# The last Q group's loads spread over stage 2, Wo copies two units later, and a weight ring that starts with five slots

## The chip, the core and the metric

The kernel runs on one core of a Trainium2 chip. The metric is the device time of one execution in microseconds; for the kernel before it is 2158.94 us, the median of six runs (2148.79 to 2162.49). The core has five engines with a queue each: TensorE (PE; its weight loads are listed as PEld), VectorE (DVE), ScalarE (ACT), GpSimd (POOL) and SyncE (SP). SP, ACT and POOL also issue DMAs, which run on 16 DMA engines that the three queues share.

## The reference

Two independent parts are computed, and their outputs stand side by side in the last dimension. Part A is a long convolution over the sequence, done with FFTs; part B is attention with a small memory that is carried from one segment of 32 positions to the next.

```python
# part A: B=1, S=2048, D=1024
kv  = shift_conv(k, shift_k) * v
y   = irfft(rfft(kv, 2S) * rfft(ssm_k, 2S))[:S]
a   = q * (y + kv * ssm_D)
# part B: Dm=1024, 32 heads of 128, memory of 8 rows
mem = mem0
for s in range(64):
    h = concat([mem, x[32*s:32*s+32]])               # 40 rows
    q, k, v = h @ Wq, h @ Wk, h @ Wv
    p = softmax(where(mask, q @ k.T * scale, -1e9))
    o = (p @ v) @ Wo
    mem, out[s] = o[:8], o[8:]
```

Each of Wq, Wk, Wv and Wo is 8 MB in bf16. They don't fit on the core together with what else is there, so a part of them is read again for every segment.

## The kernel before

**Weights in chunks.** The four matrices are cut into 64 chunks of 128 x 2048 (512 KB): eight chunks for each of two groups of K, Q and V, named (m, kc, g) with m = 0, 1, 2 and g = 0, 1, and sixteen of Wo, named (3, hp, 0). The 21 chunks of `STREAM` (L22) are streamed: early in the kernel they are copied to a scratch tensor WS in memory, and each of the 64 segments loads them from there through a ring of slots. The other chunks stay on the core (`res`). Six chunks of the last Q group, `kept_q1` (L431), get their place in the pool `pw` of eight 512 KB tiles, in tiles 4, 5, 6, 7, 0 and 1.

**Part A with part B's preparation inside it.** Stage 1 (L57 to L272) does the short convolution and the first DFT step and stores its results to SK1 and SU1. Stage 2 (L282 to L376) runs over 17 sets of rows, two halves each, 34 units in all. A set is read by four gathers on SP (`load_set` L304, tiles Kg and Ug, L289), one set ahead and with three buffers a tile; a unit then does matmuls, four products on DVE, one on POOL (Yre, L345), the inverse matmuls one unit later, and ACT stores the set to SZ (L297). Stage 3 (L378 to L399) reads SZ in 16 steps (zt) and writes part A's output.

After each unit of stage 2 and each step of stage 3 comes `fill()` (L647): it stores finished results to the scratch tensor REC (L641), issues one Wo copy from the weight to WS from unit `WO_COPY` on (L653 to L656, on POOL), one copy of other streamed chunks every second unit (L657), every third unit one block of x (`x_block`, L580: eight transposes on TensorE from X_sb, a copy on DVE into the tile xt, L589, and a store to REC on POOL, L590; a tile xt holds two blocks, so an even block's copy waits for the REC store of the block before), after every odd block the next X load (L576, on SP), and one slice of a dense projection (`dense`, L604) by `next(rest)` in two units out of three. The slices come from the generator `slices` (L619): 16 for group (0, 1), the second K group, 16 for (1, 0), the first Q group, 16 for (1, 1), the last Q group. When the generator turns to (1, 0), which is in unit 24, it issues the six loads of `kept_q1` on SP behind the last X load. Slices left over are done after stage 3, and then V's projection (L730 to L744), whose results go to the scratch tensor VBD from `vst` and `pair` tiles (L742).

**Order in the queues.** Up to the segments, a planner orders each engine's instructions at build time, by the order of the code and by when it holds an operand to be ready. `tc.issue_after(ins)` puts the instructions of a block behind `ins` on the same engine. In the segments (`tc.manual_schedule()`, L841) the order is that of the code.

**The ring.** `slot()` (L690) takes the first free of six slots; `fetch()` (L695) loads the next streamed chunk into it, on SP; `done(ch)` (L807), called after the last matmul on a chunk, frees its slot and fetches again. Slots 4 and 5 have memory of their own. Slots 0 to 3 share theirs with preparation: 0 and 1 with the transposed x (XBT), used to the end of V's projection, 2 and 3 with the `pair` tiles, of which wring2 is the one that V's last block is stored from. The order is `free = [4, 5, 0, 1, 3, 2]` (L688): two fetches stand ahead of V's projection (L727), `RING - 2` = 4 right before the segments (L842).

**A segment** does K, Q, K, Q, V, V projections of 40 rows (`Proj`, L916; the rows of x from REC), softmax, attention and Wo (`out_proj`, L1005), all from resident chunks and ring slots in the order of the chunks, and a transposition of the memory rows for the next segment. In segment 0 the streamed chunks 0 to 5 are (0,0,0), (0,1,0), (0,3,0), (0,7,0), (1,3,0) and (1,7,0); chunk 10 is (2,1,0) of V.

Of the kernel before, what the change touches and what calls it, by code (L numbers as in the profile page):

```python
# [23 lines left out]
TURN = (6, 4)  # L24
INLINE = {1: 0, 3: 1, 5: 0, 11: 1, 12: 0, 14: 1}
N2, N3 = 12, 15
WO_COPY = 27
X_LOAD, K_LOAD = 4, 2
RING = 6

PITCH = 2048


def a_kernel(ctx: ExitStack, tc, q, k, v, shift_k, ssm_k, ssm_D, outa, ps_sum, slot4, slot16, stage1_done, fill):
# [22 lines left out]
    with ExitStack() as c1:  # L57
# [183 lines left out]
        for t in range(16):  # L241
# [18 lines left out]
            for hf in range(2):  # L260
                cols = slice(512 * hf, 512 * hf + 512)
                ps = ps_sum.tile([128, 512], F32, tag="ps0", name="ks_ps")
                for li, lag in enumerate((3, 2, 1, 0)):
                    pr = wk.tile([128, 512], BF, tag="prod", bufs=10, name="prod")
# [17 lines left out]
    with ExitStack() as c2:  # L282
        gio = c2.enter_context(tc.tile_pool(name="a2_io", bufs=3, side="right"))
        wk = c2.enter_context(tc.tile_pool(name="a2_wk", bufs=3, side="right"))
        ps1 = c2.enter_context(tc.tile_pool(name="a2_ps", bufs=6, space=PSUM))

        def gather(dst, scratch, pr, eng):
            if pr <= 31:
                eng.dma_start(dst[:, :], scratch[4 * pr:4 * pr + 4].rearrange("m n d -> (m n) d"))  # L289
            else:  # L290
                eng.dma_start(dst[0:32, :], scratch[1])
                nc.gpsimd.memset(dst[32:64, :], 0.0)
                nc.gpsimd.memset(dst[64:128, :], 0.0)

# [9 lines left out]
        def load_set(st):  # L304
            prs = [2 * st, 2 * st + 1] if st < 16 else [32]
            Us, Ks = [], []
            for pi, pr in enumerate(prs):
                Kt_ = gio.tile([128, 1024], BF, tag=f"Kg{pi}", name="Kg")
                gather(Kt_, SK1, pr, nc.sync)
                Ut = gio.tile([128, 1024], BF, tag=f"Ug{pi}", name="Ug")  # L310
                gather(Ut, SU1, pr, nc.sync)
                Us.append(Ut)
                Ks.append(Kt_)
            return prs, Us, Ks
# [9 lines left out]
        def unit_front(st, prs, Us, Ks, hf):  # L324
            npart = 64 * len(prs)
            P_ = slice(0, npart)
            Kre_ps = fwd2(Ks, prs, Mre, hf, "Kre_ps")
            Kim_ps = fwd2(Ks, prs, Mim, hf, "Kim_ps")
            Kre = wk.tile([128, 512], BF, tag="Kre", name="Kre")
            Kim = wk.tile([128, 512], BF, tag="Kim", name="Kim")  # L330
            nc.scalar.copy(Kre[P_], Kre_ps[P_])
            nc.scalar.copy(Kim[P_], Kim_ps[P_])
            Ure_ps = fwd2(Us, prs, Mre, hf, "Ure_ps")
            Uim_ps = fwd2(Us, prs, Mim, hf, "Uim_ps")
            pa = wk.tile([128, 512], BF, tag="pa", name="pa")
            pb = wk.tile([128, 512], BF, tag="pb", name="pb")
            pc = wk.tile([128, 512], BF, tag="pc", name="pc")
            pd = wk.tile([128, 512], BF, tag="pd", name="pd")
            nc.vector.tensor_tensor(out=pa[P_], in0=Ure_ps[P_], in1=Kre[P_], op=ALU.mult)
            nc.vector.tensor_tensor(out=pb[P_], in0=Uim_ps[P_], in1=Kim[P_], op=ALU.mult)  # L340
            nc.vector.tensor_tensor(out=pc[P_], in0=Ure_ps[P_], in1=Kim[P_], op=ALU.mult)
            nc.vector.tensor_tensor(out=pd[P_], in0=Uim_ps[P_], in1=Kre[P_], op=ALU.mult)
            Yre = wk.tile([128, 512], BF, tag="Yre", name="Yre")
            Yim = wk.tile([128, 512], BF, tag="Yim", name="Yim")
            nc.gpsimd.tensor_tensor(out=Yre[P_], in0=pa[P_], in1=pb[P_], op=ALU.subtract)  # L345
            nc.vector.tensor_tensor(out=Yim[P_], in0=pc[P_], in1=pd[P_], op=ALU.add)
            return (Yre, Yim)
# [17 lines left out]
        for st in range(NS):  # L365
            cur = nxt
            if st + 1 < NS:
                nxt = load_set(st + 1)
            zss = [wk.tile([128, 1024], BF, tag=f"zs{pi}", name="zs") for pi in range(len(cur[0]))]
            for hf in range(2):  # L370
                Ys = unit_front(st, cur[0], cur[1], cur[2], hf)
                if pending is not None:
                    unit_back(*pending)
                pending = (st, cur[0], hf, Ys, zss)
                fill()
        unit_back(*pending)  # L376

    with ExitStack() as c3:  # L378
# [23 lines left out]
def b_kernel(ctx: ExitStack, tc, x, mem0, Wq, Wk, Wv, Wo, outb, n_seg, run_a):  # L402
# [28 lines left out]
    kept_q1 = own[1, 1][:6]  # L431
# [7 lines left out]
    def dram_chunk(ch):  # L439
        m, a, g = ch  # L440
        return Wo_v[a] if m == 3 else W_v[m][a, g]

    def dst_view(ap, ch):
        return ap.rearrange("p (hh d) -> p hh d", hh=2) if ch[0] == 3 else ap

    def stream_src(ch):
        return WS[ring_order.index(ch), :, 0:2048]
# [6 lines left out]
    res = {}  # L454
# [30 lines left out]
    def pw(k=None):  # L485
        if k is None:
            k = pw_next[0] % 8
            pw_next[0] += 1
        return pring.tile([128, 2048], BF, tag=f"pw{k}", name="pw")
# [64 lines left out]
    def group(m, g, temps={}, which=range(8), ws=None, eng=nc.sync, held=False):  # L554
        ws = ws or [None] * 8
        for kc in which:
            ch = (m, kc, g)
            if ch in res:
                got.append(eng.dma_start(res[ch], dram_chunk(ch)))
                ws[kc] = res[ch]  # L560
            else:
                t = temps[ch]() if ch in temps else pw()
                got.append(eng.dma_start(t[:], dram_chunk(ch)))
                if ch in streamed:
                    copies.append((stream_src(ch), t[:]))
                ws[kc] = t[:]
        while copies and not held:
            copied.append(nc.gpsimd.dma_start(*copies.pop(0)))
        return ws
# [23 lines left out]
    rec_stores, x_loads = [], []  # L593
# [24 lines left out]

    def slices():  # L619
        k1, q0 = group(0, 1, held=True), group(1, 0, held=True)  # L620
        q1 = [None] * 8
        first = [kc for kc in range(8) if (1, kc, 1) in kept_q1]
        rest = [kc for kc in range(8) if kc not in first]
        for m, g, ws in ((0, 1, k1), (1, 0, q0), (1, 1, q1)):
            if (m, g) == (1, 0):
                for ch, k in zip(kept_q1, (4, 5, 6, 7, 0, 1)):
                    res[ch] = pw(k)[:]
                assert not copies
                with tc.issue_after(x_loads[-1].ins):
                    group(1, 1, which=first, ws=q1)  # L630
            if (m, g) == (1, 1):
                group(1, 1, {(1, kc, 1): (lambda k=k: pw(k)) for kc, k in zip(rest, (2, 3))}, rest, q1)
            for _ in dense(m, g, ws):
                yield

    rest = slices()
    stores = []

    def store():
        if stores:  # L640
            nc.gpsimd.dma_start(*stores.pop(0))  # L641
# [2 lines left out]
    blocks = list(range(n_seg // 4))  # L644
    wo_copies = [ch for ch in ring_order if ch[0] == 3]

    def fill():  # L647
        store()
        n = units[0]
        units[0] += 1  # L650
        if n == 0:
            x_load(0)
        if n >= WO_COPY and wo_copies:  # L653
            ch = wo_copies.pop(0)
            with tc.issue_after(rec_stores[-1].ins):
                nc.gpsimd.dma_start(dst_view(stream_src(ch), ch), dram_chunk(ch))  # L656
        if n > 5 and n % 2 and copies:  # L657
            with tc.issue_after(rec_stores[-1].ins):
                copied.append(nc.gpsimd.dma_start(*copies.pop(0)))
        if n % 3 == 2 and blocks:  # L660
            b = blocks.pop(0)
            x_block(b)
            if b % 2 and blocks:
                x_load(b + 1)
        if n >= 34 or n % 3 != 2:
            next(rest, None)
# [18 lines left out]
             if s == 0 and ch not in v_temp[2:] or s > 0 and ch not in kept]  # L685
    live = {}
    now = [0]
    free = [4, 5, 0, 1, 3, 2]  # L688

    def slot():  # L690
        k = free.pop(0)
        t = (base if k < 4 else ring).tile([128, 2048], BF, tag=f"wring{k}", name="wring")
        return k, t

    def fetch():  # L695
        if loads:
            s, ch = loads.pop(0)
            live[s, ch] = k, t = slot()
            nc.sync.dma_start(t[:], stream_src(ch))
# [14 lines left out]
    with c0p:  # L714
# [15 lines left out]
        for g in range(2):  # L730
            ws = wv[g]
# [75 lines left out]
    def done(ch):  # L807
        if now[0] == 0 and ch in at_hand:
            place_late(1, at_hand[ch][1])
        elif ch in streamed:  # L810
            if now[0] == 0 and ch in kept:
                keep(ch)
            free.append(live.pop((now[0], ch))[0])
            i = order_s.index(ch)
            s, nxt = (now[0], order_s[i + 1]) if i + 1 < len(order_s) else (now[0] + 1, order_s[0])
            if nxt in kept and s > 0:
                unkeep(s, kept[nxt])
            else:
                fetch()
# [19 lines left out]
            tp[:, 0:256].rearrange("p (hf dq r) -> p dq hf r", hf=2, dq=4)[:, :, :, NX:SEG])  # L839

    with tc.manual_schedule():  # L841
        for _ in range(RING - 2):  # L842
            fetch()
        load_x(0)
        Y0 = one.tile([128, 256], BF, tag="PT", name="Y0")
# [49 lines left out]
        for s in range(n_seg):  # L895
# [143 lines left out]
            q1 = Proj(1, 1).run(4)  # L1039
# [4 lines left out]
            q1 = q1.run(4).evac()  # L1044
# [108 lines left out]
```

## Time and profile before

| What | us |
|---|---|
| median of six runs | 2158.94 |
| the profiled execution's own time | 2159.29 |
| its span, first to last instruction | 2157.5 |
| PE busy (81%) | 1752.0 |
| DVE / ACT / POOL busy | 866.4 / 637.3 / 430.0 |
| stage 2, rough window | 140 to 283 |
| stage 3, rough window | 283 to 347 |
| rest of the last Q group and V, rough window | 347 to 420 |
| segment 0, rough window | 420 to 456 |
| the other 63 segments | 456 to 2148 |

The DMA engines move 802.31 MB, 372 GB/s on the mean; 1215 ring fetches of 512 KB on SP are the largest part, with a median of 7.3 us from issue to landing. The mean granted TensorE clock is 0.98. A line of a timeline gives the start in us from the beginning of the span, the time from the first to the last of the merged instructions, the engine (SPq is SP's queue), the line of the kernel, the operation, what it writes and reads, the count, and in brackets how long the engine sat idle ahead of it and what ended that. A line of the waits gives who waited for whom, the total in us, how often, and the longest.

### The profile page before, as it was taken

Reading aid. Unit: us, or ns where it says so; the run is one execution under the profiler, and the core shown is the slowest. Engines: PE = TensorE matmul, PEld = TensorE weight load, DVE = VectorE, ACT = ScalarE, POOL = GpSimd, SP = SyncE. Lnnn points to the kernel's source line nnn. Section 1 sums busy time; section 2 is a strip of 40 time slices with the busy share of each in tenths; the row PEclk is TensorE's granted clock in tenths of the full one; section 3 lists DMA queues with packets and bytes.
Section 4 is the critical chain, followed back from the end, with each engine's and each line's share of the span. In section 5 each row is a group of like instructions: output and inputs, shape, how many; then the busy total and the mean of one; then the engine's idle time right before and its main releaser. Section 6 shows DMA issues by size and latency. Waiting matters only on the chain. (4 is left out here: it accounts for less than half of the span.)

```text
span 2157.5 us, 81579 instructions
## 1 busy us (share of the span) xinstructions
PE 1752.0 (81%) x35764; PEld 943.0 (44%) x35764; DVE 866.4 (40%) x2735; ACT 637.3 (30%) x1131; POOL 430.0 (20%) x1108
## 2 busy tenths in 40 slices
PE   6889879888888778878778888888888888887876
PEld 3433224344444444444444444444444444444444
DVE  9838652133333333333333333333333333333332
ACT  6936521122222222222222222222222222222221
POOL 3114522211111111111111111111111111111111
PEclk9999999989999999999999999999999999999999
DMA  8988989899999999999999999999999999999996
GB/s 305 370 326 309 320 297 376 289 397 392 392 389 391 384 381 389 382 389 384 377 388 394 386 385 376 389 388 382 388 386 388 391 389 390 393 392 388 386 390 266
DMA packets 238314, 802.31 MB, mean 372 GB/s; under 512 B 34722, under 2 KB 34754, under 8 KB 237956
## 3 DMA queue, kind: packets, MB, share of 16 engines
q1 hardware_dynamic: 206036, 724.01, 87.4%
q0 software_dynamic: 26704, 62.59, 8.4%
q10 hardware_dynamic: 5216, 10.49, 1.3%
q8 instruction: 280, 4.59, 0.9%
q14 instruction: 78, 0.64, 0.1%
HBM read 737.56 MB, written 62.39 MB: 371 GB/s over the span
## 5 line engine op out<-in xcount | busy, mean ns | idle before, releaser
L929 PEld LDWEIGHTS <-rec 128*32 128x32 bf16 x12351 | 325.8, 96 | 472.4 <-issue 253.9
L929 PE MATMUL acc<-wring,rec 128*32 128x512 bf16 x3765 | 377.1, 385 | 139.7 <-DMA wring<-WS 124.2
L938 ACT CAST qkv_sb<-acc 128x512 bf16<-128x512 f32 x384 | 224.8, 585 | 658.3 <-PE acc L929 655.2
L1015 PEld LDWEIGHTS <-OT 128*32 128x32 bf16 x8192 | 218.5, 97 | 172.7 <-issue 143.8
L1015 PE MATMUL yacc<-wring,OT 128*32 128x256 bf16 x3072 | 154.4, 278 | 92.5 <-DMA wring<-WS 54.2
L929 PE MATMUL acc<-Wmid,rec 128*32 128x512 bf16 x3072 | 227.5, 384 | 0.0
L929 PE MATMUL acc<-Wres,rec 128*32 128x512 bf16 x2816 | 221.2, 380 | 0.0
L875 PEld LDWEIGHTS <-OTB 128*16 128x16 bf16 x4096 | 103.9, 90 | 104.5 <-issue 94.8
L1001 ACT CAST OT<-OTp 128x512 bf16<-128x512 f32 x128 | 74.9, 585 | 244.6 <-PE OTp L993 244.4
L1031 DVE COPY KT<-tps 128x512 bf16<-128x512 bf16 x64 | 27.2, 425 | 293.5 <-PE tps L944 293.5
L1002 DVE CAST OTB<-OTp 128x128 bf16<-128x128 f32 x128 | 37.4, 292 | 263.0 <-ACT OT L1001 263.0
L830 POOL DMA_DIRECT2D rec<-REC x64 | 37.5, 586 | 526.2 <-issue 267.9
L777 DVE TENSOR_SCALAR wring<-OTp 128x384 int32<-128x384 int32 x126 | 112.3, 891 | 57.0 <-PE acc L929 46.2
L929 PE MATMUL acc<-pw,rec 128*32 128x512 bf16 x1544 | 132.0, 385 | 0.0
L905 POOL COPY KT<-rec 128x128 bf16<-128x128 bf16 x128 | 38.6, 302 | 426.7 <-PE SB L953 421.3
L959 DVE TENSOR_REDUCE mx<-SB 128x5 f32<-128x200 f32 x128 | 47.2, 368 | 185.3 <-PE SB L953 185.3
L890 POOL DMA_DIRECT2D out_dram<-YB x128 | 73.0, 577 | 236.8 <-DVE YB L888 218.8
L875 PE MATMUL SB<-wring,OTB 128*16 128x256 bf16 x1488 | 78.8, 276 | 39.1 <-DVE SB L854 32.2
L944 PEld LDWEIGHTS <-qkv_sb 128*128 128x128 bf16 x1024 | 63.0, 97 | 105.3 <-ACT qkv_sb L938 66.1
L944 PE MATMUL tps<-ident,qkv_sb 128*128 128x128 bf16 x1024 | 101.4, 222 | 8.1 <-DVE wring L777 0.2
L1015 PE MATMUL yacc<-Wlate,OT 128*32 128x256 bf16 x2048 | 105.1, 275 | 1.6 <-issue 0.9
L1071 ACT CAST Y<-yacc 128x256 bf16<-128x256 f32 x64 | 23.8, 372 | 239.1 <-PE yacc L1015 235.2
(233 smaller groups left out, 2701.8 us busy)
## 6 DMA issues: line engine op xcount, KB each, us to landing
wring<-WS SPq DMA_DIRECT2D x1215, 512.0 KB, 7.3
rec<-REC POOLq DMA_DIRECT2D x64, 192.0 KB, 6.1
SK<-s_sb SPq DMA_DIRECT2D x16, 512.0 KB, 6.5
SU<-s_sb SPq DMA_DIRECT2D x16, 512.0 KB, 7.8
Kg<-SK SPq DMA_DIRECT2D x32, 256.0 KB, 4.1
Ug<-SU SPq DMA_DIRECT2D x32, 256.0 KB, 6.2
REC<-stage POOLq DMA_DIRECT2D x16, 512.0 KB, 11.6
zt<-SZ SPq DMA_DIRECT2D x16, 512.0 KB, 7.4
```

The costliest lines, as they stand in the source:

```text
L777: nc.vector.tensor_scalar(out=dst, in0=src, scalar1=0, scalar2=None, op0=ALU.bitwise_or)
L830: nc.gpsimd.dma_start(rec[:], REC[:, s, :])
L875: nc.tensor.matmul(self.acc[32 * dq:32 * dq + W, x - o:y - o], lhsT=self.OTB[:, c, 4 * g + i, :], rhs=r, start=first and not self.seeded, ...
L890: nc.gpsimd.dma_start(bass.AP(outb.tensor, outb.offset + (SEG * NB * self.b + NX) * 2048 + 256 * dq, [[2048 * SEG, NB], [2048, 8], [1, 256 ...
L905: nc.gpsimd.tensor_copy(KT[:, :, :, 32:40], KBs[:, 128 * g:128 * g + 128].rearrange("p (c i t) -> p i c t", c=4, i=4))
L929: nc.tensor.matmul(self.acc[32 * c:32 * c + 32, x - 512 * c:y - 512 * c], lhsT=hT[:, kc, :], rhs=r, start=(kc == 0 and x == 512 * c), stop ...
L938: nc.scalar.copy(sb[:], self.acc[:])
L944: nc.tensor.transpose(tp[:, i * 128:(i + 1) * 128], sb[:, i * 128:(i + 1) * 128], ident[:])
L959: nc.vector.tensor_reduce(out=mx[:], in_=S, op=ALU.max, axis=AX.X)
L1001: nc.scalar.copy(OT[:], o_view[:, :, :, 0:32])
L1002: nc.vector.tensor_copy(OTB[:, :, 4 * g:4 * g + 4, 8 * j:8 * j + 8], o_view[:, :, :, 32:40])
L1015: nc.tensor.matmul(yacc[32 * dq:32 * dq + 32, x - o:y - o], lhsT=OT[:, c, i, :], rhs=r, start=(h == 0 and x == o), stop=(h == 31), tile_po ...
```

## The change

Four things are altered. First, four of the six `kept_q1` chunks are loaded one at a time, in the `fill()` of units 10, 13, 16 and 19, into `pw` tiles 4 to 7, each put behind the last gather that the code has issued by then (`gathers[-1]`, the last one of the next set). The last two stay in unit 24, behind the last X load, in tiles 0 and 1. Second, `WO_COPY` is 29 instead of 27, so that the six Wo copies belong to units 29 to 34; each stays behind the newest REC store of an x block on POOL. Third, slot 2 isn't among the free slots at first, and three fetches instead of four stand right before the segments. Fourth, when segment 0 is done with its streamed chunk number 4 (`LATE_SLOT`), slot 2 is added to the free slots and one more fetch is issued; from there on the ring has six slots as before.

```diff
-WO_COPY = 27
+WO_COPY = 29
+Q_LOAD = (10, 13, 16, 19)
 RING = 6
+LATE_SLOT = 4
...
+        gathers = []
+
         def gather(dst, scratch, pr, eng):
             if pr <= 31:
-                eng.dma_start(dst[:, :], scratch[4 * pr:4 * pr + 4].rearrange("m n d -> (m n) d"))
+                gathers.append(eng.dma_start(dst[:, :], scratch[4 * pr:4 * pr + 4].rearrange("m n d -> (m n) d")))
             else:
-                eng.dma_start(dst[0:32, :], scratch[1])
+                gathers.append(eng.dma_start(dst[0:32, :], scratch[1]))
...
-                fill()
+                fill(gathers[-1])
...
         k1, q0 = group(0, 1, held=True), group(1, 0, held=True)
-        q1 = [None] * 8
...
             if (m, g) == (1, 0):
-                for ch, k in zip(kept_q1, (4, 5, 6, 7, 0, 1)):
-                    res[ch] = pw(k)[:]
                 assert not copies
-                with tc.issue_after(x_loads[-1].ins):
-                    group(1, 1, which=first, ws=q1)
+                for kc, k in zip(first[4:], (0, 1)):
+                    q1_load(kc, k, x_loads[-1].ins)
...
+    q1 = [None] * 8
     rest = slices()
...
-    def fill():
+    def q1_load(kc, k, ins):
+        res[1, kc, 1] = pw(k)[:]
+        with tc.issue_after(ins):
+            group(1, 1, which=[kc], ws=q1, held=True)
+
+    def fill(behind=None):
...
+        if n in Q_LOAD:
+            i = Q_LOAD.index(n)
+            q1_load(kept_q1[i][1], 4 + i, behind.ins)
...
-    free = [4, 5, 0, 1, 3, 2]
+    free = [4, 5, 0, 1, 3]
...
             i = order_s.index(ch)
+            if now[0] == 0 and i == LATE_SLOT:
+                free.append(2)
+                fetch()
...
-        for _ in range(RING - 2):
+        for _ in range(RING - 3):
             fetch()
```

## The prediction

> **What bounds the kernel now.** I read the busy time by stage first (windows cut where the work changes), then each engine's timeline around the windows in which TensorE is short of work, then the DMA queue's own waits at the start of the segments. Columns of the windows: PE, PEld, DVE, ACT, POOL busy us (instructions), granted clock, DMA share, GB/s.
>
> ```profile
> 230.00:283.00 53.00, 44.02 (x219) 14.58 (x217) 36.65 (x62) 25.44 (x49) 29.23 (x30) 0.87 0.85 301
> 283.00:347.00 64.00, 47.06 (x213) 20.08 (x213) 25.02 (x27) 5.85 (x10) 14.62 (x18) 0.92 0.97 363
> 347.00:420.00 73.00, 71.77 (x333) 32.47 (x332) 11.18 (x18) 16.38 (x28) 19.45 (x24) 1.00 0.95 330
> 420.00:456.00 36.00, 24.81 (x472) 12.32 (x469) 10.65 (x38) 7.97 (x14) 3.26 (x12) 0.79 0.90 335
> 456.00:2148.00 1692.00, 1366.93 (x33517) 782.60 (x33515) 613.18 (x2205) 432.69 (x819) 297.30 (x943) 0.99 1.00 386
> ```
>
> From 456 us on the DMA engines are full (share 1.00) and 63 segments take 26.86 us each; nothing in the change alters a segment after the first, so what is won or lost before 456 us moves the end one for one. Before that, the V part (347 to 420) is TensorE's, stage 3 (283 to 347) the DMA engines', and the two places with slack on both are the end of stage 2 and segment 0. There the timelines of SP, DVE, PE and POOL show:
>
> ```profile
> 231.55 9.94 SPq L559 DMA_DIRECT2D pw<-in_B_Wq_dram  x6
> ...
> 257.05 0.40 SPq L576 DMA_DIRECT2D X_sb<-in_B_x_dram  x1
> ...
> 247.57 0.69 DVE L589 COPY xt<-xt_ps 128x1024 bf16<-128x1024 bf16 x1 [8.73 <-DMA REC<-xt]
> ...
> 248.31 1.44 PE L610 MATMUL kb_ps<-XBT,Wmid 128*128 128x512 bf16 x3 [4.97 <-DVE xt L589]
> ...
> 266.96 0.29 PE L587 MATMUL xt_ps<-ident,X_sb 128*128 128x128 bf16 x1 [2.50 <-DMA X_sb<-in_B_x_dram]
> ...
> 253.43 2.03 POOL L656 DMA_DIRECT2D WS<-in_B_Wo_dram  x3
> ```
>
> Six 512 KB loads in a row hold SP for 9.94 us. In their backlog the REC store of x block 7 (issued at 235.16) lands 12.3 us later instead of the 5.5 of the five before it; block 8's copy on DVE waits for it, and TensorE stands 4.97 us (**gap 1**). The X load for block 10 is issued late, beside three Wo copies, and lands 9.9 us after its issue (others: 6.6): 2.50 us (**gap 2**). After each gap the clock is at half:
>
> ```profile
> 248.00:251.00 3.00, 2.69 (x7) 0.99 (x7) 3.00 (x6) 0.00 (x0) 1.37 (x2) 0.50 1.04 386
> 251.00:254.00 3.00, 3.00 (x15) 0.58 (x12) 3.00 (x7) 1.07 (x2) 2.17 (x3) 0.63 1.02 391
> ...
> 266.00:269.00 3.00, 2.04 (x11) 0.86 (x12) 0.02 (x1) 1.13 (x3) 1.90 (x3) 0.64 0.81 238
> 269.00:272.00 3.00, 3.00 (x15) 0.69 (x12) 2.89 (x5) 0.93 (x2) 1.15 (x1) 0.50 0.88 318
> 272.00:275.00 3.00, 3.00 (x13) 0.83 (x13) 1.75 (x4) 1.22 (x3) 0.05 (x1) 0.72 0.33 124
> ```
>
> Busy time times the missing clock: 2.69 x 0.50 + 3.00 x 0.37 = 2.5 us after gap 1, 2.04 x 0.36 + 3.00 x 0.50 + 3.00 x 0.28 = 3.1 us after gap 2. Whole price: 7.4 and 5.6 us. In segment 0, SP's waits, a PE line and the windows:
>
> ```profile
> SPq L699 <- DMA VBD<-pair: 7.8, 1, 7.8
> ...
> 432.61 0.62 PE L929 MATMUL acc<-wring,rec 128*32 128x512 bf16 x4 [2.30 <-DMA wring<-WS]
> ...
> 422.00:424.00 2.00, 1.69 (x28) 0.66 (x21) 0.00 (x0) 0.00 (x0) 0.84 (x1) 1.00 0.80 213
> 424.00:426.00 2.00, 0.00 (x0) 0.00 (x0) 0.00 (x0) 0.00 (x0) 0.00 (x0) 1.00 0.70 258
> 426.00:428.00 2.00, 1.39 (x20) 0.56 (x19) 0.00 (x0) 0.58 (x1) 0.00 (x0) 0.82 0.89 328
> 428.00:430.00 2.00, 2.00 (x20) 0.79 (x17) 0.42 (x1) 0.00 (x0) 0.00 (x0) 0.50 0.05 16
> 430.00:432.00 2.00, 0.31 (x4) 0.00 (x0) 0.00 (x0) 0.00 (x0) 0.00 (x0) 0.50 0.83 274
> ```
>
> SP's sixth ring fetch, into slot 2, waits 7.8 us for the last VBD store out of that memory; all later fetches stand behind it while the DMA engines run dry (share 0.05).
>
> **The change part by part.** No instruction is added or removed; six loads, six copies and one slot move. The sum is made against the profiled execution's 2159.29 us (span 2157.5), 0.35 us over the median of 2158.94.
>
> *Ring.* Fetches 0 to 4 go out as before (the last at 421.0). Fetch 5 now takes the slot that chunk 0 frees at about 422.2, 6 and 7 follow within 1.5 us, and the wait for the VBD store passes to fetch 10, whose chunk is used only in the V projection, near 440. Behind that wait stand fetches 11 and on; the backlog then holds five chunks of 1.34 us (512 KB at 390 GB/s), 6.7 us from 427.7, so it may last to 434 unseen; the store landed at 429.2 and may come a few us later beside more loads. The gain is the idle share from 422 to 432 against 1.03 of a full window: (0.23 + 0.33 + 0.14 + 0.98 + 0.20) x 2 = 3.8 us. Ends: 0 (slot 2 held just as long, seen elsewhere) and 7.8 (the whole wait). I take 3.7, the row that is nearest: the rest of the kernel is DMA time.
>
> *Four Q chunks behind the gathers of units 10, 13, 16 and 19.* The SP timeline has those gathers end at 172.7, 180.4, 195.5 and 202.1. Each load costs SP 0.3 to 0.5 us and the DMA engines 1.34. SP's next instruction comes 5 us later or more, so nothing stands behind them there. Cover: the share falls to 0.30 in 176 to 179, 0.82 in 179 to 182, 0.79 in 200 to 203, 0.39 in 206 to 209. The tightest user is block 4's copy on DVE at 200.07, which needs block 3's store of 190.57; at the 5.5 us of its like that leaves 4 us. Cost 0; if the cover fails, the price of a gap, 5.6 to 7.4.
>
> *The burst at 231 us is two loads instead of six.* SP gets through to the gathers of sets 14 and 15 at 233 and 238 instead of 241.7 to 253, and the DMA engines, full from 231 to 264, are relieved of 2 MB, 5.4 us. For gap 2 this counts whole: the X load is issued some 2 us sooner with one Wo copy (not three) beside it, at 6.6 us lands at about 262, and is wanted at 264.5. Gain 5.6, ends 0 and 5.6. For gap 1 it counts little: the gathers that stood behind the loads now fill SP's queue in the same time (0.5 MB X, 1 MB Wq, 1.5 MB gathers up to 247), so the store still shares the engines. The row nearest is the store's own 12.3 us landing against 5.5; DVE would have to get it 5 us sooner. Ends 0 and 7.4; I take 1.0, because the traffic named above stays.
>
> Two rules are weighed here. The Trainium skill, "DMA: Bandwidth & Descriptors", Queues, rings and completion order, says that each DMA engine goes round the queues that have work, a packet from each. By that, POOL's store keeps its share whatever SP's backlog is and gap 1 would stay whole: the sum would be 1.0 us less gain; shared by bytes in order of issue, the store would come 5.4 us sooner and gap 1 go, 6.4 us more. The skill's "TensorE: Matmul & The Clock Gate", Why this matters for your kernels, asks for idle gaps under about 3 us to keep the clock; the 2.50 us of gap 2 in the row above did lose it. By the rule gap 2 would be worth 2.5 us, the sum 3.1 less; the row decides.
>
> *Wo copies two units later.* Before, three copies stood behind block 8's REC store and three behind block 9's on POOL; now one, three and two behind block 10's. POOL's cost is 0.55 to 0.88 us each, between the Yre products that TensorE needs, in idle stretches of 1.1 and 1.6 us there. The two last copies move 1 MB, 2.7 us of DMA time, where the share is 0.14 to 0.47 (275 to 281) but just ahead of the last SZ stores that stage 3 waits for. Cost between -2.7 (idle filled that stage 3 would pay) and +2.8; I take +0.8, as the copies would start after 280, where the share is 0.89 and more, and the dip at 287 to 290 (0.25) gives 2.2 us back.
>
> Sum: -3.7 - 5.6 - 1.0 + 0 + 0.8 = -9.5: **2149.8 us**.
>
> **The rivals.**
> 1. Both gaps go. DVE's copy of block 8 stands one unit ahead of where the code puts it; the planner that orders the queues may place it later once the burst is smaller, or the store lands sooner. Against it: the backlog is refilled by gathers. All 7.4 of gap 1 for the 1.0 in the sum, 6.4 us more: 2143.4.
> 2. Only the ring pays: another wait takes gap 2's place (X is issued only when block 9 has left its buffer, whatever the queue), or stage 3, at DMA share 0.97, gives the gain back. For it: the bytes are the same. Against it: in 272 to 281 the engines stood at 0.14 to 0.47, so stage 2's end isn't their bound. -3.7 + 0.8: 2156.4.
> 3. Slower. An early Q load delays a REC store past DVE's next xt copy, as at 247.57, in the middle of stage 2 (blocks 2, 4, 6 at 179, 200, 222 us). Each costs 7.4 us, so one leaves 2157.2, two make 2164.6, slower than before. The point: a landing more than 4 us longer than 5.5. One load adds 1.34 us, which speaks against it; the engines at 1.03 and more from 182 to 197 speak for it.
> That the loads don't spread is excluded, for each is ordered behind its gather on SP.
>
> **How the numbers follow.** Forecast 0.53, rival 1 0.15, rival 2 0.21, rival 3 0.11. The forecast's own range is 2145 to 2154 (gap 1 half gone; ring 1 us less with copies 2 us dearer). Adding rivals 1 and 2 gives 2142 to 2160; outside lie rival 3 with two gaps and the best of rival 1. A change under 0.3% (6.5 us) can't be told from none here. Faster (under 2152.5): 0.39 of the forecast, 0.15, 0.03 of rival 2: 0.57. Slower (over 2165.4): 0.07 from rival 3. Same: 0.36.
>
> **What would show it.** Ring: no SP wait on VBD<-pair ahead of TensorE's line of 432.61, whose 2.30 us wait is gone, and no DMA share under 0.7 between 422 and 432 (shifted). Burst: two Wq loads behind X at about 231, four single ones before 205; no wait on X_sb at about 264 and no half clock behind it; DVE's wait on REC<-xt still several us. Copies: a 1-3-2 pattern on POOL; stage 3's first zt load less than 7 us after the last SZ store. I am wrong if a new wait of DVE on REC<-xt or of PE on X_sb stands between 170 and 230, or if stage 3 grows by what stage 2 lost.

## The result and the profile after

The changed kernel takes 2149.17 us (median of 37 runs), the kernel before 2157.13 us (81 runs beside it). The ratio is 0.9962, with a 95% interval of 0.9952 to 0.9972: 8.2 us less, between 6.0 and 10.4. 8.2 us is more than the 6.5 us (0.3%) under which the prediction calls a change not told from none; the near end of the interval is a little less.

The two profiled executions lie further apart: 2145.51 us after, 2159.29 us before, spans of 2142.9 and 2157.5. Of those 14.6 us, 2.2 were already there when set 6 was gathered (168.10 instead of 170.27 us), ahead of everything that the change touches, and 3.4 come after the first output store of segment 0, in a stretch whose length differs by up to 11 us between executions of kernels with the same segments. The 9.0 us between lie where the change acts. A second execution of each kernel (e5 and e12 below) is 7.3 us apart there, so the mean of the two pairs is 8.2. So I compare stretches, not ends.

Busy time by stage, same windows and columns as before (PE, PEld, DVE, ACT, POOL busy, granted clock, DMA share, GB/s), kernel after:

```profile
230.00:283.00 53.00, 47.05 (x233) 16.31 (x232) 35.80 (x63) 25.81 (x49) 28.04 (x30) 0.94 0.85 285
283.00:347.00 64.00, 47.18 (x225) 20.74 (x223) 26.04 (x29) 5.85 (x10) 15.12 (x19) 0.97 0.99 367
347.00:420.00 73.00, 67.43 (x347) 30.37 (x345) 9.52 (x16) 15.21 (x26) 19.94 (x27) 1.00 0.94 328
420.00:456.00 36.00, 28.69 (x579) 14.26 (x575) 12.20 (x41) 9.41 (x17) 4.52 (x18) 0.86 1.03 400
```

From 230 to 283 us TensorE is busy for 47.05 us instead of 44.02 and at 0.94 of its clock instead of 0.87. From 420 to 456 us the DMA engines move 400 GB/s instead of 335. These are the two places that the prediction named. (The windows are fixed in time, and the kernel after is 2 us ahead at 230 and 11 us at 456.) The timelines around block 8 of x, kernel after:

```profile
229.13 1.00 SPq L563 DMA_DIRECT2D pw<-in_B_Wq_dram  x2
230.18 3.18 SPq L293 DMA_DIRECT2D Ug<-SU  x2
...
252.11 0.40 SPq L580 DMA_DIRECT2D X_sb<-in_B_x_dram  x1
...
243.62 0.69 DVE L593 COPY xt<-xt_ps 128x1024 bf16<-128x1024 bf16 x1 [7.20 <-DMA REC<-xt]
...
244.36 0.81 PE L614 MATMUL kb_ps<-XBT,Wmid 128*128 128x512 bf16 x3 [2.03 <-DVE xt L593]
```

SP is through with the Wq loads, now two, after 1.0 us (9.94 before, for six), and the two Ug gathers of set 14 follow at once, at 230.18. In the timeline of SP before they stood behind the burst:

```profile
241.68 2.56 SPq L289 DMA_DIRECT2D Ug<-SU  x2
```

X of block 10 goes out at 252.11 and is waited for nowhere near 264. DVE still waits 7.20 us for block 7's REC store, which landed 10.8 us after its issue (12.3 before), but TensorE now lost 2.03 us by it instead of 4.97. The clock was lost all the same, windows of the kernel after:

```profile
245.00:248.00 3.00, 2.84 (x9) 0.74 (x8) 3.00 (x6) 0.00 (x0) 1.88 (x2) 0.56 1.03 350
248.00:251.00 3.00, 3.00 (x13) 0.66 (x10) 2.36 (x5) 1.32 (x3) 2.57 (x3) 0.50 0.82 291
251.00:254.00 3.00, 3.00 (x20) 1.40 (x18) 1.88 (x4) 2.06 (x5) 1.86 (x3) 0.80 0.89 259
```

SP's wait for the VBD store around segment 0, in the waits of the kernel after (total us, times, longest):

```profile
SPq L709 <- DMA VBD<-pair: 3.1, 1, 3.1
```

The windows of the kernel after that answer to 422 to 430 before, since segment 0 starts 7.25 us sooner:

```profile
415.00:417.00 2.00, 1.44 (x24) 0.55 (x17) 0.00 (x0) 0.00 (x0) 0.59 (x1) 1.00 0.85 272
417.00:419.00 2.00, 1.05 (x16) 0.45 (x16) 0.00 (x0) 0.53 (x1) 0.00 (x0) 1.00 0.84 264
419.00:421.00 2.00, 1.15 (x20) 0.60 (x20) 0.39 (x1) 0.06 (x1) 0.00 (x0) 1.00 1.00 399
421.00:423.00 2.00, 1.66 (x31) 0.66 (x24) 0.04 (x1) 0.58 (x1) 0.00 (x0) 1.00 1.03 389
```

The wait shrank from 7.8 to 3.1 us and comes at fetch 10 (issued at 423.86), as forecast, instead of fetch 5. The stretch at share 0.05 is gone, the lowest of these windows is 0.84, and the clock is whole in them.

**Stretches of all profiles.** One table serves the rest. "To SZ" runs from the issue of set 6's gather (about 170 us, where no kernel differs yet) to the issue of the last SZ store, the end of stage 2; "to zt" from there to stage 3's first zt load; "segment 0" from its first matmul to its first output store. Block 8, Kre and X_sb are TensorE's idle times ended by block 8's copy on DVE, by ACT's Kre copy and by the X load, between 230 and 283 us (only those of 1 us and more; the 1.34 of after and the 1.65 of e10 stand at 283 and 281 us and are for block 12, all others for block 10). Each row is one profiled execution; three of one and the same stage 2 (before, e5, e1) lie up to 4 us apart. The ratios are to the kernel before, timed on the same chip; a difference in us is the ratio times the median of before there, 2156 to 2158 us.

| kernel | ratio [95%] | block 8 | Kre | X_sb | to SZ | to zt | segment 0 |
|---|---|---|---|---|---|---|---|
| before | 1 | 4.97 | - | 2.50 | 114.6 | 4.1 | 34.2 |
| e5 before, again | - | 3.61 | 1.37 | 2.82 | 112.6 | 4.3 | 33.4 |
| e1 ring alone | 0.9990 [0.9970, 1.0011] | 3.32 | 2.36 | - | 110.6 | 4.3 | 30.2 |
| e3 Wo alone | 1.0001 [0.9983, 1.0019] | 4.02 | 1.34 | - | 109.6 | 5.2 | 33.4 |
| e2 Q alone | 0.9972 [0.9951, 0.9993] | - | 1.53 | 1.21 | 106.7 | 4.5 | 33.1 |
| e4 Q and Wo | 0.9966 [0.9946, 0.9985] | - | 1.55 | - | 107.2 | 5.1 | 34.1 |
| after | 0.9962 [0.9952, 0.9972] | 2.03 | - | 1.34 | 109.2 | 5.3 | 30.2 |
| e12 after, again | 0.9950 [0.9930, 0.9971] | 1.70 | 1.44 | - | 107.3 | 5.3 | 30.4 |
| e6 after, last two Q loads later | 0.9961 [0.9945, 0.9977] | 2.16 | - | - | 106.5 | 5.3 | 30.3 |
| e7 before, one xt buffer | 1.0003 [0.9985, 1.0021] | - | 10.94 | - | 115.4 | 4.0 | 34.4 |
| e8 after, one xt buffer | 0.9963 [0.9943, 0.9983] | - | 1.19, 1.52 | - | 105.1 | 5.5 | 31.0 |
| e9 before, burst behind the gathers | 0.9973 [0.9953, 0.9993] | - | - | - | 106.1 | 4.5 | 34.0 |
| e10 e6 and e8 together | 0.9978 [0.9957, 0.9998] | - | - | 2.92, 1.65 | 107.1 | 5.7 | 30.6 |
| e11 e10, Wo from unit 27 | 0.9957 [0.9942, 0.9972] | - | - | 3.59 | 107.2 | 4.2 | 30.5 |

### The profile page after: what moved, and what is told of

Same layout as the page of the kernel before. It is cut to its first block, busy times and chain, and to the rows that moved or that the text cites. A ratio compares the mean times of both kernels' runs of the same rounds, so it can differ in the third digit from the quotient of the medians.

```text
span 2142.9 us, 81577 instructions
## 1 busy us (share of the span) xinstructions
PE 1741.9 (81%) x35764; PEld 939.7 (44%) x35764; DVE 865.6 (40%) x2735; ACT 637.4 (30%) x1131; POOL 430.1 (20%) x1108
## 5 line engine op out<-in xcount | busy, mean ns | idle before, releaser
L942 PE MATMUL acc<-pw,rec 128*32 128x512 bf16 x1544 | 131.2, 382 | 0.0
L888 PE MATMUL SB<-wring,OTB 128*16 128x256 bf16 x1488 | 79.3, 275 | 37.6 <-DVE SB L867 30.6
## 6 DMA issues: line engine op xcount, KB each, us to landing
REC<-stage POOLq DMA_DIRECT2D x16, 512.0 KB, 10.5
```

What stands on the lines that cost most here:

```text
L888: nc.tensor.matmul(self.acc[32 * dq:32 * dq + W, x - o:y - o], lhsT=self.OTB[:, c, 4 * g + i, :], rhs=r, start=first and not self.seeded, ...
L942: nc.tensor.matmul(self.acc[32 * c:32 * c + 32, x - 512 * c:y - 512 * c], lhsT=hT[:, kc, :], rhs=r, start=(kc == 0 and x == 512 * c), stop ...
```

## The experiments

Theory at the start: the gain is the sum of three parts that do not touch each other: ring (segment 0), Q loads (block 8 and block 10 in stage 2), Wo copies (a small cost ahead of stage 3). The rival: one part carries it all. The first four runs do one part or two alone.

**e1, the ring alone.** The kernel before with

```
+LATE_SLOT = 4
...
-    free = [4, 5, 0, 1, 3, 2]
+    free = [4, 5, 0, 1, 3]
...
+            if now[0] == 0 and i == LATE_SLOT:
+                free.append(2)
+                fetch()
...
-        for _ in range(RING - 2):
+        for _ in range(RING - 3):
```

> Only the ring starts with five slots and takes the sixth after chunk 4; Q loads and Wo copies as in the kernel before. Theory (the parts add): stage 2 stays as it was with both gaps (DVE's wait of about 8 us, TensorE's waits of about 5.0 and 2.5 us), segment 0 gets 3.7 us shorter, and the whole time falls by 3.7 us, ratio 0.9983. The trace would show fetch 5 issued about 1 us after fetch 4 instead of 8, no 2.3 us TensorE wait for it, and the VBD wait passed to fetch 10. Rival (the ring is the whole change, and what stage 2 shows is run to run): the time falls by 8 us, ratio 0.996. Other rival (DMA time of the later fetches only moves): no change, 0.9995 to 1.0005.

Measured: -2.2 us (-6.5 to +2.4), too wide to decide by itself. Segment 0 decides: 30.2 us, against 33.1 to 34.4 in the seven profiles without the ring's change and 30.2 to 31.0 in the seven with it. The means are 33.8 and 30.5: the ring is worth 3.3 us.

What e1 also shows: its stage 2 has the program of before, burst and all, and no wait on X_sb. The timeline of TensorE in e1:

```profile
245.24 1.44 PE L611 MATMUL kb_ps<-XBT,Wmid 128*128 128x512 bf16 x3 [3.32 <-DVE xt L590]
...
254.63 0.41 PE L320 MATMUL Kre_ps<-Kg,Mre 128*64 128x512 bf16 x2 [2.36 <-ACT Kre L332]
```

**e2, the Q loads alone.** The changed kernel, with the Wo copies and the ring of before:

```
-WO_COPY = 29
+WO_COPY = 27
...
-LATE_SLOT = 4
...
-    free = [4, 5, 0, 1, 3]
+    free = [4, 5, 0, 1, 3, 2]
...
-            if now[0] == 0 and i == LATE_SLOT:
-                free.append(2)
-                fetch()
...
-        for _ in range(RING - 3):
+        for _ in range(RING - 2):
```

> Only the four Q loads are spread; Wo copies at unit 27 and six ring slots as in the kernel before. Theory (the burst makes both gaps late): the X load of block 10 is issued 2 us or more sooner, the 2.5 us wait for it is gone though three Wo copies still run beside it, DVE's wait for the REC store of block 7 stays at 6 us or more; 5.5 us less, ratio 0.9975. Rival (the Wo copies are what holds the X load up): the 2.5 us wait and its half clock stay, only 1 to 2 us less, ratio 0.999 to 0.9995.

Measured: -6.0 us (-10.6 to -1.5). To the end of stage 2: 106.7 us against 110.6 to 114.6 for the three profiles with stage 2 as before, whose mean is 112.6. The spread is the largest part; the value of the rival (1 to 2 us) lies inside the interval of the whole, but not near the 5.9 us of the stretch.

**e3, the Wo copies alone.** The kernel before with

```
-WO_COPY = 27
+WO_COPY = 29
```

> Only the Wo copies start at unit 29; the burst of six Q loads and six ring slots as in the kernel before. Theory (the burst makes both gaps): the X load for block 10 is still issued late, behind the burst and the gathers; its wait shrinks by at most 1.5 us; the two last copies cost 0.8 us at the turn to stage 3; in all -1.5 to +0.8 us, ratio 0.9993 to 1.0004. Rival (the Wo copies hold the X load up): the 2.5 us wait goes with its 3.1 us of half clock, 4.8 us less, ratio 0.9978.

Measured: +0.2 us (-3.7 to +4.1). From the last SZ store to the first zt load 5.2 us instead of 4.1 to 4.3. The X_sb wait is gone here (under 1 us), as the rival said, but the 4.8 us that it set on that are not there; and e1 lacks the wait too, with the Wo copies where they were.

**e4, Q and Wo without the ring.** As e2, but with the Wo copies of the changed kernel:

```
-WO_COPY = 27
+WO_COPY = 29
```

> The whole change without its ring part: Q loads spread, Wo copies at unit 29, six slots from the start. Theory (the parts add): what the change wins less the ring's 3.7 us, so 4.3 us less than before, ratio 0.998; segment 0 again has the 7.8 us wait for the VBD store and TensorE's 2.3 us. Rival (stage 3 is a DMA stage and gives the gain back, and only the ring pays): within 1 us of before, ratio 0.9995 to 1.0005.

Measured: -7.3 us (-11.6 to -3.2), segment 0 as before (34.1 us). The theory had 4.3. With the ring's 3.3 us it would make -10.6, against the changed kernel's -8.2; the two agree within e4's interval. Wo's later copies cost in every kernel that has them from unit 29: 5.1 to 5.7 us to the first zt load, against 4.0 to 4.5 from unit 27. By the means (5.33 and 4.27) the copies cost 1.1 us there.

**e5, the kernel before once more.** The X_sb wait of before was missing in e1 and e3. Was it chance?

> The kernel before, once more. Ring and Wo alone (the two runs in which the Q loads are still a burst of six) showed the stall of block 8 (3.32 and 4.02 us on TensorE) but not the X_sb wait of 2.50 us at about 267. Theory: that X_sb wait belonged to the one execution that was profiled, so here X_sb holds TensorE for under 1.2 us, and block 8's copy for 3 to 5 us. Rival: it belongs to this combination of burst and early Wo copies, so it is here again with 2 us or more.

The timeline of TensorE in e5:

```profile
249.91 1.04 PE L610 MATMUL kb_ps<-XBT,Wmid 128*128 128x512 bf16 x3 [3.61 <-DVE xt L589]
...
258.37 0.41 PE L319 MATMUL Kre_ps<-Kg,Mre 128*64 128x512 bf16 x2 [1.37 <-ACT Kre L331]
...
269.46 0.23 PE L587 MATMUL xt_ps<-ident,X_sb 128*128 128x128 bf16 x1 [2.82 <-DMA X_sb<-in_B_x_dram]
```

It is here again, so "chance" falls. But e1, with the same stage 2, does not have it. Of three executions of that program two wait on X_sb, two on Kre, and all three on block 8: one backlog, whose price is put down to a different waiter each time. The theory, that this wait belonged to one execution, was wrong, and so is the rival's reading that the program always has it. What no single line tells is what the backlog as a whole delays.

**e6, the last two Q loads later too.** The changed kernel with

```
-Q_LOAD = (10, 13, 16, 19)
+Q_LOAD = (10, 13, 16, 19, 30, 31)
...
-                for kc, k in zip(first[4:], (0, 1)):
-                    q1_load(kc, k, x_loads[-1].ins)
...
-            q1_load(kept_q1[i][1], 4 + i, behind.ins)
+            q1_load(kept_q1[i][1], (4, 5, 6, 7, 0, 1)[i], behind.ins)
```

> The changed kernel, with the last two Q loads (those behind X at about 229 us) behind the gathers of units 30 and 31 instead, at about 252; all else in the same order. Theory (what is left of block 8's stall comes from what SP queued ahead): 1 MB or 2.7 us less stands beside block 7's REC store, so it lands 8 us after its issue instead of 10.8, block 8's copy waits about 4.5 us instead of 7.2, TensorE's 2.03 us and the half clock behind it are gone: 3 to 5 us faster than the changed kernel. Rival 1 (POOL's own 512 KB stage stores and the gathers hold the store): landing within 1 us of 10.8, time within 1 us of the changed kernel. Rival 2: the loads now fall beside the Wo copies and X of block 10: a wait on X_sb of 2 us or more, 2 to 5 us slower.

Measured: block 7's store landed after 9.47 us, between theory (8) and rival 1 (10.8); block 8's stall stayed, in the timeline of TensorE in e6:

```profile
247.78 0.81 PE L614 MATMUL kb_ps<-XBT,Wmid 128*128 128x512 bf16 x3 [2.16 <-DVE xt L593]
```

The time is that of the changed kernel (-8.4 us against before, -11.9 to -5.0; the changed kernel -8.2). The theory's 3 to 5 us are not there, nor is rival 2's wait on X_sb.

**e7, the burst without block 8's wait.** The kernel before with one xt tile for all blocks, its halves written in turn, so that block 8's copy needs block 6's store, landed long ago, and not block 7's. Every engine's order stays.

```
-        if b % 2 == 0:
+        if b == 0:
             t = base.tile([128, 2048], BF, tag="wring3", name="xt")
-            xts[b], xts[b + 1] = t[:, 0:1024], t[:, 1024:2048]
+            for i in range(n_seg // 4):
+                xts[i] = t[:, 1024 * (i % 2):1024 * (i % 2) + 1024]
```

> The kernel before, with one xt buffer for all blocks, so that block 8's copy waits for block 6's REC store (landed at 227) and no longer for block 7's; every engine's order is that of before, the burst of six loads stays. Theory (the burst costs time only by way of block 8's copy): TensorE's 3 to 5 us at block 8 and the half clock behind it (2.5 us) are gone, 4 to 7 us faster than before, stage 2 from block 7's store to the last SZ store 43 to 45 us instead of 45 to 50. Rival (the burst costs time by its bytes, or the gathers behind it become the next wait): less than 2 us faster, with a new wait of TensorE on Kre or Ure (gathers) or of SP in its place.

Measured: +0.6 us (-3.2 to +4.5). The copy no longer waits, block 8's REC store goes out at 239.64 us, 8 us after block 7's instead of 15.6, and nothing is won. Timelines of e7:

```profile
228.15 10.16 SPq L559 DMA_DIRECT2D pw<-in_B_Wq_dram  x6
238.37 3.02 SPq L289 DMA_DIRECT2D Ug<-SU  x2
...
255.54 0.58 ACT L331 CAST Kre<-Kre_ps 128x512 bf16<-128x512 f32 x1 [12.23 <-DMA Ug<-SU]
...
256.18 0.64 PE L319 MATMUL Kre_ps<-Kg,Mre 128*64 128x512 bf16 x2 [10.94 <-ACT Kre L331]
```

Windows of e7:

```profile
248.00:251.00 3.00, 0.00 (x0) 0.00 (x0) 0.00 (x0) 0.00 (x0) 0.00 (x0) 0.62 1.02 401
251.00:254.00 3.00, 0.00 (x0) 0.00 (x0) 0.00 (x0) 0.00 (x0) 0.00 (x0) 0.50 1.04 416
```

The Ug gather behind the six loads is issued at 238.37 and lands at 255.04, 16.7 us later. ACT's queue stands until then and TensorE behind it, while the DMA engines are full (1.02 to 1.04). The rival holds in its second form: the burst delays the gathers behind it in SP's queue, and block 8's copy had hidden that wait.

**e8, the changed kernel with the same edit.** Again

```
-        if b % 2 == 0:
+        if b == 0:
...
-            xts[b], xts[b + 1] = t[:, 0:1024], t[:, 1024:2048]
+            for i in range(n_seg // 4):
+                xts[i] = t[:, 1024 * (i % 2):1024 * (i % 2) + 1024]
```

> The changed kernel with the same edit. Theory: what the changed kernel has left of block 8's stall (2.03 us and 3 us of half clock) is gone as well, 3 to 5 us faster than the changed kernel; and since the burst then has no copy to hold up, the distance to the kernel before with this edit is that of ring and Wo alone, 1.5 to 4 us. Rival: the spread of the Q loads pays by another way than block 8's copy, and the distance is 6 us or more. Rival 2: TensorE waits at the same place for the next thing (gathers, X of block 10), and this edit is worth under 1 us.

The timeline of TensorE in e8:

```profile
243.27 0.41 PE L323 MATMUL Kre_ps<-Kg,Mre 128*64 128x512 bf16 x2 [1.19 <-ACT Kre L335]
...
253.22 0.41 PE L323 MATMUL Kre_ps<-Kg,Mre 128*64 128x512 bf16 x2 [1.52 <-ACT Kre L335]
```

Here the edit clears block 8 and no long wait takes its place: 105.1 us to the end of stage 2, the shortest of all, 2.3 to 4.1 less than the two profiles of the changed kernel. But the whole is not measurably faster (-8.0 us, -12.3 to -3.7). And the distance from e7 to e8 is 8.6 us, not the 1.5 to 4 us of ring and Wo. Their intervals leave room for less, but the stretches to the end of stage 2 do not: 115.4 against 105.1 us. With block 8's wait out of both kernels, spreading the loads (here with the later Wo copies) is worth no less than with it. It does not pay by way of block 8's copy; TensorE's wait on Kre, 10.94 us in e7 and at most 1.52 here, says that it pays by the gathers.

**e9, the burst kept together, but behind the gathers.** If the order in SP's queue is the cause, six loads in a row should cost nothing where no gather stands behind them. e2's kernel, which has the ring and the Wo copies of before, with all six loads behind the gathers of units 30 and 31:

```
-Q_LOAD = (10, 13, 16, 19)
+Q_LOAD = (30, 31)
...
-                for kc, k in zip(first[4:], (0, 1)):
-                    q1_load(kc, k, x_loads[-1].ins)
...
-            i = Q_LOAD.index(n)
-            q1_load(kept_q1[i][1], 4 + i, behind.ins)
+            for i in range(3) if n == 30 else range(3, 6):
+                q1_load(kept_q1[i][1], (4, 5, 6, 7, 0, 1)[i], behind.ins)
```

> The kernel before, with its burst of six Q loads kept together, three behind the gathers of unit 30 and three behind those of unit 31, which is behind all gathers of stage 2 on SP (at about 250 us instead of 231); ring and Wo as before. Theory (the burst costs because gathers of the last two sets and block 7's store stand behind and beside it, whether it is spread or not): block 8's stall at most 2 us, no wait of TensorE on Kre over 2.5 us, and from set 6's gather to the last SZ store 106 to 109 us as with the spread (106.7 and 107.2), not the 110.6 to 115.4 of the kernels with the burst at 231: time as Q alone, 4 to 7 us under before. Rival (its bytes cost wherever they lie together): 3 MB or 8 us of DMA time now hold X of block 10 and the Wo copies, TensorE waits on X_sb 3 us or more, or the first zt load comes later; time within 2 us of before.

Measured: -5.8 us (-10.1 to -1.5), as Q alone. Timelines of e9 and its window:

```profile
231.23 0.95 SPq L292 DMA_DIRECT2D Ug<-SU  x2
...
251.65 9.72 SPq L562 DMA_DIRECT2D pw<-in_B_Wq_dram  x6
...
243.99 0.81 PE L613 MATMUL kb_ps<-XBT,Wmid 128*128 128x512 bf16 x3 [0.92 <-DVE xt L592]
```

```profile
230.00:283.00 53.00, 46.72 (x254) 17.34 (x255) 39.02 (x66) 26.80 (x52) 30.32 (x32) 1.00 0.96 339
```

SP spends 9.72 us on the burst again, the same bytes lie in the same window (share 0.96, the highest of all), and TensorE keeps its clock at 1.00 throughout; to the end of stage 2 it is 106.1 us. Spreading was not needed; taking the loads from in front of the gathers was.

Since the burst is also 20 us later here (251.65 instead of 231.55), one rival is left: its bytes cost because of when they move, not because of the queue. The landings of all fourteen profiles speak against it. Counted from set 6's gather, the second Ug gather of set 14 lands after 85.3 to 85.9 us with six loads in front of it on SP (89.7 in e7), after 77.7 to 79.0 with two (after, e12, e2, e4, e8), and after 71.0 to 72.0 with none (e6, e9, e10, e11). Block 7's REC store, on POOL's queue in the same backlog, lands 10.6 to 12.3, 9.4 to 10.8 and 8.2 to 10.2 us after its issue. So 3 MB moved the transfer in the same queue by 14 us and the one in another queue by 2.

**e10 and e11, everything together.** e10 is the changed kernel with e6's and e8's edits, e12 the changed kernel as it is, and e11 is e10 with

```
-WO_COPY = 29
+WO_COPY = 27
```

> The changed kernel with one xt buffer (block 8's copy no longer waits for block 7's store) and the last two Q loads behind the gathers of units 30 and 31: both things that stood behind the rest of the burst are free. Theory: from set 6's gather to the last SZ store 104 to 106 us (the changed kernel 109.2, its stage 2 without the ring 107.2), and the whole 2 to 4 us under the changed kernel timed beside it. Rival: what stage 2 wins, stage 3 gives back (DMA share 0.95 and more from 283 to 347), and the whole is within 1 us of it.

> The same with the Wo copies from unit 27 again, as before. Theory: from the last SZ store to the first zt load 4.1 to 4.5 us instead of 5.1 to 5.3, and about 1 us less in all than with the copies from unit 29. Rival: three copies in a row beside X of block 10 bring the X_sb wait back, 2 to 3 us, and the whole is 1 to 2 us slower than with unit 29.

> The changed kernel, once more, timed on the same chip as the three others. Theory: 2149 us; a stall of 1.5 to 3.5 us at block 8 again and no X_sb wait over 1.5 us at about 264; from the first matmul of segment 0 to the first output store 30 to 31 us, with no SP wait on the VBD store ahead of the sixth fetch. If the X_sb wait is here, its absence from the first profile was chance.

Measured: e10 -4.7 us (-9.3 to -0.4), e11 -9.3 us (-12.5 to -6.0), e12 -10.8 us (-15.1 to -6.3). No combination beats the changed kernel; e10's intervals reach too far to call it slower. e10's theory failed twice, with 107.1 us to the end of stage 2 instead of 104 to 106 and no gain on the whole. The X_sb wait is back in e10 (and in e11, 3.59 us); the timeline of TensorE in e10:

```profile
258.26 0.23 PE L592 MATMUL xt_ps<-ident,X_sb 128*128 128x128 bf16 x1 [2.92 <-DMA X_sb<-in_B_x_dram]
```

With block 8 and 9 free sooner, X of block 10 is issued at 245.88 instead of 252.11, but into the full engines: it lands 12.3 us later, and TensorE is there before it. e11's first zt load comes 4.2 us after the last SZ store, as expected from the earlier copies; its X_sb wait is the rival's, but it isn't slower than e10 for it. In e12 the changed kernel again has no X_sb wait of 1 us; its stall at block 8 is 1.70 us, in the timeline of e12:

```profile
246.50 0.81 PE L614 MATMUL kb_ps<-XBT,Wmid 128*128 128x512 bf16 x3 [1.70 <-DVE xt L593]
```

## Why the prediction was right, and where it was not

The time (2149.8 forecast, 2149.17 measured) came out nearer than the gain: 9.5 us forecast from an execution at 2159.29, 8.2 measured from a median of 2157.13. That it fits to 0.6 us is luck: the burst was priced too high, the median of before lay 2.2 us below the execution that the sum starts from, and part of the gain stands in no term. By steps:

- **Ring, -3.7.** Right: -3.3 in segment 0. The wait went to fetch 10, and no window ran dry behind it. Of the two waits of TensorE on ring chunks in segment 0 (2.54 and 2.30 us before, 1.80 and 3.94 in e5) at most one over 1.5 us is left: the second, 2.30 us before, is nowhere over 1.5 us, the first still takes 2.5 to 2.8 us in e8, e10, e11 and e12.
- **Four Q loads behind earlier gathers, 0.** Right. From set 6's gather to block 6's REC store it is 52.8 and 52.6 us in the two profiles of before, 52.6 and 52.6 in those of after: no wait appeared between 170 and 223 us, so rival 3 falls.
- **The burst, -5.6 for gap 2 and -1.0 for gap 1.** This step was too large, and its reason was in part wrong. To the end of stage 2 the mean of the three profiles with the old stage 2 is 112.6 us, of the changed one (after, e12, e4) 107.9: -4.7 instead of -6.6. The 5.6 us had been read off one execution's X_sb wait as if it were the program's; e1 ran the same stage 2 without it. Gap 1 had been priced low because the gathers would fill SP's queue in the loads' place. The store indeed gained little (see e9), and of the 4.7 us only 0.8 had been won when block 8's copy started; 3.9 come behind it, where 5.6 were forecast. TensorE's stall at block 8 fell from between 3.3 and 5.0 us to 2.0, 1.7 and 0.95 (after, e12, e4), but part of that only moved: 0.9 to 1.6 us on Kre now stand some 5 us ahead of it. What was taken for mere traffic, the gathers of sets 14 and 15, was what the burst held up: e7 shows their wait at 10.94 us when nothing hides it, e9 that the same burst behind them costs stage 2 nothing that shows (106.1 us, 106.7 with it spread).
- **Wo copies, +0.8.** Near in size, not in its reason: +1.1 between the last SZ store and the first zt load, but the last two copies went out at 266.85 and 268.55 us, not after 280, and why the first zt load then comes later no run shows. Whether the later copies save as much inside stage 2 the runs cannot tell: e3 is shorter there than the old stage 2 (109.6 against 112.6), e4 not shorter than e2.
- **Rival 1** (both gaps gone, 6.4 us more): the time did not come, though the gaps nearly went. Block 8 still costs 2.03 us and the clock in the first profile, but 1.70 and 0.95 us with the clock whole in e12 and e4. The two gaps had been priced at 13.0 us together; in these two, stage 2 is about 7.3 us shorter than in that execution and about 5.4 shorter than the mean of three. So the prices of gaps that one backlog makes don't add up. **Rival 2** (only the ring pays) falls with e2 and e9.
- The sum of the measured steps, -3.3 - 4.7 + 1.1 = -6.9 us, lies inside the measured interval; 1.3 us of the median's 8.2 are not assigned.

What stays open: to the end of stage 2, e6 and e8 are shorter than the changed kernel, and yet not faster. No stage ahead of the segments takes that back: from the first zt load to segment 0 it is 131.2 and 131.8 us in them, 132.0 and 132.7 in the two profiles of the changed kernel. But behind segment 0's first output store come 1697 to 1707 us, among the seven profiles with the new ring, and the intervals of the whole are about 4 us each way, so a gain of 2 to 4 us would not show.

## What to carry to other kernels

A burst of loads on a queue costs by what stands behind it in that queue, so put it behind the transfers that are wanted next; in this kernel it then mattered little whether it was spread (e9). Before a wait in a profile is priced, ask what the same engine would wait for next: with block 8's copy freed, e7 waited 10.94 us for the gathers and won nothing. And a wait seen in one execution is not yet the program's: look at stretches over several executions, because one backlog shows as a different waiter each time.

## What the runs showed of the hardware

- **The clock.** Between 150 and 292 us the fourteen profiles hold 43 idle gaps of TensorE of 1 to 3 us. None of the 21 below 2.0 us was followed by a granted clock under 1.00; of the 22 from 2.0 us on, 18 were followed by half clock, as the 2.03 us above (the longest that kept the clock, in e4, took 2.63). The Trainium skill, "TensorE: Matmul & The Clock Gate", Why this matters for your kernels, asks for gaps under about 3 us; here the limit lay at 2, and not sharply. A cut from 4.97 to 2.03 us therefore won the gap but not the clock, and 1.70 us (e12) kept it.
- **Two queues share, one queue waits.** The late landings under e9 are mostly a late issue: with six loads ahead the second Ug gather of set 14 goes out about 12 us later than with none, and from issue to landing it takes 11.6 to 15.8 us instead of 9.2 to 10.5. With two loads ahead it goes out 2 us later than with none and then takes 14.1 to 14.8, so its time from issue to landing alone does not tell what the burst costs. Block 7's store on POOL's queue took 11.4 us on the mean with six loads beside it, 10.0 with two and 9.4 with none: 3 MB, 8 us of DMA time (an estimate from 512 KB at 390 GB/s), moved it by 2 us. That is nearer to what the Trainium skill's "DMA: Bandwidth & Descriptors", Queues, rings and completion order, says of queues taken in turn than to a share in order of issue.
